# A gated attention unit and a low-rank mixer on one core: order of the start, of the first loads and of the turns of x + h

## The chip, the cores and the metric

The kernel runs on one core of one Trainium2 chip. The metric is the device time of one execution in microseconds; of several executions the median counts, and lower is better.

## The reference

Eight batches of 3136 rows; u and v have 256 columns, z has 64. All inputs and the output are float32.

```python
scores = z @ z.transpose(0, 2, 1) / 3136
attn   = np.maximum(scores, 0.0) ** 2
x      = u * (attn @ v)                                  # gated attention
h      = (x.transpose(0, 2, 1) @ U @ V).transpose(0, 2, 1)  # U: 3136 x 32, V: 32 x 3136
y      = x + h
out    = y + np.maximum(y @ w_ch1, 0.0) @ w_ch2          # w_ch1: 256 x 1024, w_ch2: 1024 x 256
```

The scores are symmetric, so a block of scores that has been computed serves a second time when it is transposed.

## The kernel before

**Tiles.** The 3136 rows of a batch are 24 tiles of 128 rows and a tail of 64. Four tiles make a group, so a batch has six whole groups (g = 0 to 5) and a small one (g = 6). An item is (batch, group), 56 in all. TensorE works in bfloat16 with the 128 rows of its array split into two halves of 64 that run at the same time (`pair`, L177; its matmuls have line 182 in the profile). PSUM is handed out as four tiles of two banks (`take_ps`, L146): a product that finds none free waits until ACT or DVE has read one.

**Scores.** The scores of group g against group J are a block of 512 x 512, made in two jobs, each one pair of matmuls (`score_pairs`, L424). ACT or DVE takes a pair out of PSUM (scale and relu, `rectify`, L364: lines 376, 382, 386, 393) and DVE squares it in place (`square`, L360, line 362; in the start ACT squares one, line 377). Blocks lie in 20 buffers (`take_block`, `give_block`). A block (J, g) with J > g is used by item g as it is, and by item J after a transpose by a DMA on SP's queue (`issue_turn`, L403: line 416, and line 408 for the half of a diagonal block). In batch 0 most are made twice instead of transposed. Which engine takes a pair is chosen by booked times (`book`, `free_at`).

**Slots.** One slot is one item's attention product with v (`av_stream`, L631, 96 units of two matmuls), with which the slot's other work is interleaved by place numbers (`emit`, L1094): score jobs of a later group (`todo`), z's turns in the start, the mixer's parts for an item seven or eight slots earlier. In slot t, x = u * (attn @ v) of item t is made (`av_out`, line 734). After a batch's last item, `t1_all` (L777, lines 782 to 796) makes x^T U for the whole batch. From then on `u2_unit` (L808) makes x + h for one item: a product with V into PSUM, the sum on DVE (line 855), a cast to bfloat16 (`down`, through `cast`, L199: line 202 on ACT, 204 on DVE), and a transpose by DMA (`turned`, `x_turn`, L767: line 770, "u2T<-x_bf"). The first channel product (`ch1_part`, L906; relu at 943 or 946) needs that transpose; the second (`ch2_stream`, L994) follows, and `ch2_out` (L1059, lines 1066 and 1068) adds and stores.

**The planner.** All of this is an instruction order worked out while the program is built. `clock` counts TensorE's planned time in units of one pair of 256 columns; `hold(due, f)` keeps a step until the planner's clock has reached `due`, and `run_held` (L122) lets out what is due. The same function then lets out block transposes from `ready_turns`, the soonest needed first, as long as `urgent` is empty and SP's booked time allows it. `urgent` holds an item whose turn of x + h shall go first; `turned` clears it. Before the change only `u2_unit` with g = 0 sets it. A product that needs a block whose transpose has not been let out issues it on the spot. Each engine executes its instructions in the order in which they were issued.

**Loads.** All DMAs go through SP's queue. z and v of the next batch are loaded in float32 into three stages and cast a slot later (`load_part`, L271; casts held in `casts_next`). U, V and the two weights are loaded once, in the slots that `first_loads` names, into attention blocks lent for it (`stage_block`); V comes in four steps of four DMAs, each weight in two steps of one. In slots 0 to 7 the loads of a slot are held 5, 27, 49, ... units after its beginning.

**The start.** z of batch 0 comes in three pieces. Each is cast twice and turned by matmuls with an identity (`z_turn`, L323, line 329), which ACT copies to `zzT` (line 338). `warm` puts matmuls of the identity on itself in front (line 327). Score pairs 0 and 1 need the first turned piece (tiles 0 to 3), pairs 2 and 3 the second (tiles 4 to 7); tiles 8 to 15 come with the third.

Of the kernel before, what the change touches and what calls it, by code (L numbers as in the profile page):

```python
# [18 lines left out]
def kernel(  # L19
# [13 lines left out]
    B, S, D = u.shape  # L33
# [10 lines left out]
    GT = 4  # L44
# [10 lines left out]
    NG = len(groups)  # L55
# [21 lines left out]
    NQ = NF // GT  # L77
# [18 lines left out]
    clock = [0.0]  # L96
# [4 lines left out]
    urgent = []  # L101
# [9 lines left out]
    def book(eng, ready, cost):  # L111
        free_at[eng] = max(free_at[eng], ready) + cost
        return free_at[eng]
# [5 lines left out]
    def hold(due, f):  # L119
        held.append((due, len(held), f))  # L120
# [18 lines left out]
    def pe(cost):  # L139
        clock[0] += cost  # L140
# [3 lines left out]
    ps_free = [0.0] * NPS  # L144

    def take_ps():  # L146
        k = min(range(NPS), key=lambda i: ps_free[i])
        assert ps_free[k] < float("inf")
        clock[0] = max(clock[0], ps_free[k])
        ps_free[k] = float("inf")  # L150
        for bank in range(2):
            wrote.pop((k, bank), None)
        return k, ps_pool.tile([P, 2, GW], FP32, name=f"ps{k}")
# [45 lines left out]
    def cast(out, in_, n):  # L199

        if free_at["act"] <= free_at["dve"]:
            nc.scalar.copy(out=out, in_=in_)  # L202
            return book("act", clock[0], n / 110)
        nc.vector.tensor_copy(out=out, in_=in_)  # L204
        return book("dve", clock[0], n / 130)
# [117 lines left out]
    def z_turn(b, t0, copy, n=2 * GT, warm=0):  # L323
        n = min(n, NT - t0)
        k, pz = take_ps()
        for _ in range(warm):
            nc.tensor.matmul(out=pz[:, 0, :P], lhsT=ident, rhs=ident, start=True, stop=True)  # L327
        for q in range(n):
            nc.tensor.matmul(  # L329
                out=pz[:, q // GT, (q % GT) * P : (q % GT + 1) * P],  # L330
                lhsT=z_bfs[b][:, t0 + q, :, :].rearrange("p c d -> p (c d)"),
                rhs=ident,
                start=(q % GT == 0),
                stop=(q % GT == GT - 1 or q == n - 1),
            )
        flat = pz.rearrange("p a c -> p (a c)")
        dst = zzTs[b].rearrange("p t c -> p (t c)")[:, t0 * P : (t0 + n) * P]
        copy(out=dst, in_=flat[:, : n * P])
        pe(8)
        ps_free[k] = book("act", clock[0] + 3, 9.5)  # L340


    def half(zzT, jj, c0, n):
# [383 lines left out]
    def four(ps):  # L727
        return ps.rearrange("p a (q d) -> p (a q) d", d=D)
# [79 lines left out]
    def u2_unit(b, g, turn=True):  # L808
        ts = tiles_of(g)
        n, t0, rows = len(ts), ts[0][1], ts[0][2]  # L810
        k, ps = take_ps()
        if n == GT:
            for a in range(2):
                pair(
                    k,
                    crossed(
                        0,
                        a,
                        lambda h, q: dict(
                            out=four(ps)[:, q, :],  # L820
                            lhsT=V4_bf[h, (t0 + q) * P : (t0 + q + 1) * P],
                            rhs=t1s[b][h, :],
                            start=(a == 0),
                            stop=(a == 1),
                        ),
                    ),
                    D,
                )
        else:
            pair(  # L830
                k,
                [
                    (
                        0,
                        0,
                        dict(
                            out=ps[:, 0, :D],
                            lhsT=V4_bf[:hp, t0 * P : (t0 + 1) * P],
                            rhs=t1s[b][:hp, :],
                            start=True,  # L840
                            stop=True,
                        ),
                    )
                ],
                D,
            )
        x = xs[b, g][:rows, :n, :]
        if b == B - 1:
            entry, raw = stage_block()
            o_blocks[b, g] = entry  # L850
            o = raw.rearrange("p (q d) -> p q d", d=D)
        else:
            o = pool.tile([P, GT, D], FP32, name="out_sb", bufs=3)
        done = ps_free[k] = book("dve", clock[0] + 3, 11.2 * n / GT)
        nc.vector.tensor_tensor(out=o[:rows, :n, :], in0=four(ps)[:rows, :n, :], in1=x, op=ALU.add)  # L855
        u2s[b, g] = o
        if not turn:
            return

        def turned():  # L860
            u2Ts[b, g] = u2T_tile()
            x_turn(b, g, u2Ts[b, g])
            urgent.clear()

        def down():
            hold(cast(x, o[:rows, :n, :], n * D) + 2, turned)

        if g == 0:
            urgent.append((b, g))
            nc.vector.tensor_copy(out=x, in_=o[:rows, :n, :])  # L870
            hold(book("dve", done, 6.3) - 6, turned)
        else:
            hold(done - 3, down)
# [293 lines left out]
    def load_w(k):  # L1167
        def step(i):
            entry, raw = stage_block()
            if k == 0:  # L1170
                nc.sync.dma_start(out=raw, in_=moe_w_ch1[i * P : (i + 1) * P, :])
                dst = w1_bf[:, i, :]
            else:
                nc.sync.dma_start(
                    out=raw.rearrange("p (t d) -> p t d", d=D),
                    in_=moe_w_ch2.rearrange("(t p) d -> p t d", p=P)[:, i * GT : (i + 1) * GT, :],
                )
                dst = w2_bf[:, i * GT : (i + 1) * GT, :].rearrange("p t d -> p (t d)")
            queued(GT * D / 2)

            def casts(entry=entry, raw=raw, dst=dst):
                cast(dst, raw, GT * D)
                give_block(entry)

            return [casts]

        return [lambda i=i: step(i) for i in range(2)]


    def load_V(i0):  # L1190
        n = P // 4

        def step(i):
            entry, raw = stage_block()
            w = n * NF + (S - NF * P if i == 3 else 0)
            for c in range(NREP):
                nc.sync.dma_start(out=raw[c * R : (c + 1) * R, :w], in_=moe_V[:, i * n * NF : i * n * NF + w])  # L1197
                queued(w / 8)

            def casts(i=i, entry=entry, raw=raw):  # L1200
                cast(
                    V4_bf[:, : NF * P].rearrange("r (t p) -> r t p", p=P)[:, :, i * n : (i + 1) * n],
                    raw[:, : n * NF].rearrange("r (p t) -> r t p", t=NF),
                    2 * n * NF,
                )
                if i == 3:
                    nc.vector.memset(V4_bf[:, S:], 0.0)
                    cast(V4_bf[:, NF * P : S], raw[:, n * NF : n * NF + S - NF * P], 100)
                give_block(entry)

            return [casts]

        return [lambda i=i: step(i) for i in range(i0, i0 + 2)]


    first_loads = {
        1: lambda: load_V(0),
        2: lambda: load_V(2),
        3: lambda: [load_U],
        4: lambda: load_w(0),  # L1220
        5: lambda: load_w(1),
    }


# [5 lines left out]
    on_act, on_dve, on_pool = nc.scalar.copy, nc.vector.tensor_copy, nc.gpsimd.tensor_copy  # L1230
# [51 lines left out]
    k, ps = take_ps()  # L1282
# [6 lines left out]
        cast_z(0, c, on_dve, GT, 2 * GT)  # L1289
    for i in range(2):  # L1290
        give_block(zraw[i][2])
    clock[0] = 38
    z_turn(0, 0, on_act, GT)
    z_turn(0, GT, on_act, GT)
    clock[0] = 43
    free_at.update(dve=46, act=47)
    jobs0 = jobs_of(0, 0)
    score_burst(jobs0[:1])
    score_burst(jobs0[1:2])
    clock[0] = 56  # L1300
    z_turn(0, 2 * GT, on_act, warm=10)
    score_burst(jobs0[2:3])
    score_burst(jobs0[3:4])
    clock[0] = 72

    todo = {t: [] for t in range(n_items)}
    for b in range(B):
        for g in range(NQ):
            t = b * NG + g - 1
# [12 lines left out]
            else:  # L1322
                todo[t] += new

    for t, most in ((0, 15), (1, 16), (2, 13)):
        todo[t + 1] = todo[t][most:] + todo[t + 1]
        todo[t] = todo[t][:most]

# [5 lines left out]
    for t in range(n_items):  # L1334
# [6 lines left out]
        g_now = t % NG  # L1341
        b_next = t // NG + 1
# [6 lines left out]
            xTs[direct] = take_block()[1][:, : GT // 2, :].rearrange("p a (q d c) -> p (a q) d c", d=ND, c=P)  # L1349
            x_turn(*direct, xTs[direct])  # L1350
        for i, f in enumerate(casts_next):
            hold(clock[0] + (90 if g_now == NQ else 15 if t > NG else 45) + 12 * i, f)
        casts_next = []
        spare += spare_next
        spare_next.clear()
        steps = first_loads[t]() if t in first_loads else []
        if b_next < B:
            steps += load_part(b_next, g_now)

        def load(step):  # L1360
            casts_next.extend(step())
# [35 lines left out]
        if av and full:  # L1397
# [5 lines left out]
            n = len(mine) - 3  # L1403
            qs += [(9 + 74 * i / n, 1, False, lambda: scores(1)) for i in range(n)]
        elif av:
# [5 lines left out]
            k = min(2, len(mine) // 3)  # L1411
            n = len(mine) - 3 * k
            at = [1 + 80 * i / n for i in range(n)]
            if t == 0:
                at, k = [14, 30, 44, 50, 64, 68, 78, 84, 92], 0
# [101 lines left out]
```

## Time and profile before

| | |
|---|---|
| median of three runs | 986.9 us (986.28 to 986.96) |
| the profiled execution | 988.19 us, span 986.4 us |
| PE (matmul) busy | 974.8 us, 99% of the span |
| DVE, ACT, POOL busy | 627.8, 483.6, 16.6 us |
| packets of the hardware DMA queue | 86.9% of 16 engines' span |
| granted TensorE clock | 1.0 |

PE is the matmul engine, PEld its weight loads, DVE the vector engine, ACT the scalar engine, SP the engine whose queue issues the DMAs. Lines of the profile carry the line of the kernel that issued an instruction, and what it writes and reads as out<-in, buffer numbers left out. A row of the timeline begins with the start and the duration in us; in brackets stands the idle time of the engine before it and what ended that. An SP row of a DMA is the time that its issue took, not its transfer. In this trace slot 0 begins near 9 us, slots 1 to 6 near 26, 44, 56, 69, 84 and 94 us, slot 7 near 96 us and slot 8 near 112 us; then a slot takes some 17 us.

### The profile page before, as it was taken

To read this page: it belongs to the slowest core of one execution; us is meant where nothing else is said; L and a number is where in the kernel's file an instruction comes from. 1 tells how busy PE (TensorE), PEld (TensorE's weight loads), DVE (VectorE), ACT (ScalarE), POOL (GpSimd) and SP (SyncE) were. 2 spreads that over 40 slices of the span, in tenths; PEclk is the share of its full clock that TensorE was granted. 3 is DMA by queue.
4 is the path that set the end of the run, shared out by engine and by line. 5 is a ranking of instruction groups with operands and counts; after the bars stand their busy time and mean duration, and the time that the engine had idled before them with its cause. 6 is when DMAs were issued, how large, how long until landed. Compare 5 with 4: busy or idle time off the path is not lost.

```text
span 986.4 us, 35362 instructions
## 1 busy us (share of the span) xinstructions
PE 974.8 (99%) x16165; PEld 780.2 (79%) x16165; DVE 627.8 (64%) x809; ACT 483.6 (49%) x562; POOL 16.6 (2%) x25
## 2 busy tenths in 40 slices
PE   9999999999999999999999999999999999999998
PEld 6798788877778778787777877788777887778766
DVE  7877755668556685567755667566775567653363
ACT  7887732456324573345633555334554346431353
POOL 4100000000000000000000000000000000000000
PEclk9999999999999999999999999999999999999999
DMA  9999999979997699897999679997899878954143
GB/s 264 208 252 181 205 205 199 197 155 190 203 192 174 151 196 217 205 151 171 180 224 209 135 178 195 227 184 137 171 214 224 179 136 167 193 121 100 49 113 99
DMA packets 372405, 176.37 MB, mean 179 GB/s; under 512 B 347296, under 2 KB 350624, under 8 KB 372256
## 3 DMA queue, kind: packets, MB, share of 16 engines
q1 hardware_dynamic: 372256, 174.12, 86.9%
q8 instruction: 126, 2.06, 0.9%
q14 instruction: 23, 0.19, 0.1%
HBM read 62.56 MB, written 25.69 MB: 89 GB/s over the span
## 4 chain that ended last, share of the span: by engine, by line
PE 94%; DVE 2%; ACT 2%; DMA 1%; SPq 1%; issue 0%; DVEq 0%; POOL 0%; POOLq 0%
PE ps L182 91%; DVE blk L362 1%; PE ps L701 1%; DMA u2T<-x_bf 1%; ACT blk L386 1%; PE ps L782 1%; PE ps L1080 0%; SPq L416 0%; DVE blk L382 0%; PE ps L1284 0%; ACT blk L946 0%; PE ps L329 0%; SPq L1197 0%; PE ps L327 0%; DVE x_bf L734 0%
## 5 line engine op out<-in xcount | busy, mean ns | idle before, releaser
L182 PEld LDWEIGHTS <-blk 64*128 64x128 bf16 x12288 | 615.6, 94 | 153.6 <-POOLq L172 9.9
L182 PE MATMUL ps<-v_bf,blk 64*128 64x256 bf16 x9216 | 612.1, 269 | 1.9 <-ACT v_bf L202 1.8
L386 ACT ACTIVATE blk<-ps 128x1024 bf16<-128x1024 f32 (+1 forms) x334 | 314.8, 972 | 346.4 <-PE ps L182 341.6
L362 DVE TENSOR_TENSOR blk<-blk 128x1024 bf16<-128x1024 bf16 x351 | 223.1, 660 | 46.8 <-ACT blk L386 46.1
L182 PE MATMUL ps<-u2T,w_bf 64*128 64x512 bf16 (+1 forms) x1792 | 227.8, 349 | 1.6 <-DMA u2T<-x_bf 1.5
L182 PE MATMUL ps<-w_bf,blk 64*128 64x256 bf16 x3072 | 192.4, 269 | 0.2 <-ACT blk L946 0.2
L943 DVE TENSOR_SCALAR blk<-ps 128x1024 bf16<-128x1024 f32 x105 | 128.5, 1224 | 94.5 <-PE ps L182 93.9
L946 ACT ACTIVATE blk<-ps 128x1024 bf16<-128x1024 f32 x87 | 88.3, 1022 | 118.3 <-PE ps L182 118.0
L182 PE MATMUL ps<-zzT 64*128 64x512 bf16 (+2 forms) x902 | 130.8, 328 | 1.3 <-ACT blk L386 0.5
L182 PEld LDWEIGHTS <-w_bf 64*128 64x128 bf16 x1792 | 84.6, 94 | 28.8 <-POOLq L172 5.0
L734 DVE TENSOR_TENSOR x_bf<-ps,u_sb 128x1024 bf16<-128x1024 f32 x48 | 58.6, 1222 | 72.3 <-PE ps L182 72.2
L855 DVE TENSOR_TENSOR out_sb<-ps,x_bf 128x1024 f32<-128x1024 f32 x42 | 51.4, 1223 | 59.5 <-PE ps L182 59.5
L1066 DVE TENSOR_TENSOR out_sb<-ps,out_sb 128x1024 f32<-128x1024 f32 x42 | 51.4, 1224 | 18.7 <-PE ps L182 18.3
L182 PEld LDWEIGHTS <-zzT 64*128 64x128 bf16 x902 | 41.8, 94 | 7.3 <-issue 2.7
L382 DVE TENSOR_SCALAR blk<-ps 128x1024 bf16<-128x1024 f32 (+1 forms) x14 | 16.1, 1147 | 11.0 <-PE ps L182 10.1
L182 PE MATMUL ps<-t_sb,V_bf 64*128 64x256 bf16 x200 | 20.6, 269 | 0.0
L204 DVE CAST v_bf<-stage 128x1024 bf16<-128x1024 f32 (+1 forms) x33 | 20.2, 611 | 0.0
L182 PE MATMUL ps<-v_bf,last_sb 64*128 64x256 bf16 x192 | 18.5, 269 | 0.2 <-POOLq L172 0.2
L202 ACT CAST v_bf<-stage 128x1024 bf16<-128x1024 f32 x15 | 15.6, 1043 | 0.0
L204 DVE CAST x_bf<-out_sb 128x1024 bf16<-128x1024 f32 x21 | 14.5, 688 | 0.3
L202 ACT CAST x_bf<-out_sb 128x1024 bf16<-128x1024 f32 x14 | 14.5, 1037 | 0.0
L362 DVE TENSOR_TENSOR attn_small<-attn_small 128x1600 bf16<-128x1600 bf16 x8 | 7.9, 991 | 9.0 <-ACT attn_small L591 9.0
(80 smaller groups left out, 240.6 us busy)
## 6 DMA issues: line engine op xcount, KB each, us to landing
u_sb<-in_u_dram SPq DMA_DIRECT2D x48, 512.0 KB, 5.2
stage<-in_v_dram SPq DMA_DIRECT2D x42, 512.0 KB, 6.2
out_dram<-out_sb SPq DMA_DIRECT2D x42, 512.0 KB, 3.1
stage<-in_z_dram SPq DMA_DIRECT2D x7, 512.0 KB, 6.1
blk<-in_v_dram SPq DMA_DIRECT2D x5, 512.0 KB, 6.1
out_dram<-blk SPq DMA_DIRECT2D x5, 512.0 KB, 2.6
blk<-blk SPq DMA_TRANSPOSE x156, 5.1
blk<-in_moe_w_ch_dram SPq DMA_DIRECT2D x4, 512.0 KB, 4.7
```

Of the source, the lines that this page charges most:

```text
L182: ins = nc.tensor.matmul(**args)
L202: nc.scalar.copy(out=out, in_=in_)
L204: nc.vector.tensor_copy(out=out, in_=in_)
L362: nc.vector.tensor_tensor(out=a, in0=a, in1=a, op=ALU.mult)
L382: nc.vector.tensor_scalar(out=dst, in0=src, scalar1=scale, scalar2=0.0, op0=ALU.mult, op1=ALU.max)
L386: nc.scalar.activation(out=dst, in_=src, func=AF.Relu, scale=scale)
L701: nc.tensor.matmul(out=ps[c * hp : c * hp + rows, h, :D], lhsT=smalls[b][h * hp : (h + 1) * hp, place_of(jt), :], rhs=v_bfs[b][h * hp : (h ...
L734: nc.vector.tensor_tensor(out=xs[b, g][:rows, :n, :], in0=four(box["ps"])[:rows, :n, :], in1=u_sbs[b, g][:rows, :n, :], op=ALU.mult,)
L855: nc.vector.tensor_tensor(out=o[:rows, :n, :], in0=four(ps)[:rows, :n, :], in1=x, op=ALU.add)
L943: nc.vector.tensor_single_scalar(out=r, in_=ps[:, :, :gw], scalar=0.0, op=ALU.max)
L946: nc.scalar.activation(out=r, in_=ps[:, :, :gw], func=AF.Relu)
L1066: nc.vector.tensor_tensor(out=o, in0=acc, in1=o, op=ALU.add)
```

## The change

It has five edits, all to the order of issue or to the planner's numbers; what is computed and each instruction's shape stay.

- `u2_unit`: an item with g > 0 now also enters `urgent` when its sum is cast, until its turn has been issued; block transposes are held back for that time.
- The start: pairs 2 and 3 are issued ahead of z's third turn; its ten warm matmuls go, and four are put ahead of the second turn. The planner counts a short turn as short.
- `first_loads`: V's two pairs of steps move from slots 1 and 2 to 3 and 4, U from 3 to 2, the weights from 4 and 5 to 5 and 6. Within a slot v's loads go ahead of them.
- Casts of what was loaded a slot before: in slot 6 from 90 to 15 units after the slot's beginning, in slot 7 from 45 to 15.
- The score jobs at most issued in slots 0, 1 and 2: 15, 16, 13 become 14, 15, 14; what is over goes to the next slot.

```diff
@@ z_turn @@
-        pe(8)
-        ps_free[k] = book("act", clock[0] + 3, 9.5)
+        pe(n)
+        ps_free[k] = book("act", clock[0] + 3, 9.5 * n / (2 * GT))
@@ u2_unit @@
         def down():
+            urgent.append((b, g))
             hold(cast(x, o[:rows, :n, :], n * D) + 2, turned)
@@ first_loads @@
-        1: lambda: load_V(0),
-        2: lambda: load_V(2),
-        3: lambda: [load_U],
-        4: lambda: load_w(0),
-        5: lambda: load_w(1),
+        2: lambda: [load_U],
+        3: lambda: load_V(0),
+        4: lambda: load_V(2),
+        5: lambda: load_w(0),
+        6: lambda: load_w(1),
@@ the start @@
-    clock[0] = 38
+    clock[0] = 32
     z_turn(0, 0, on_act, GT)
-    z_turn(0, GT, on_act, GT)
+    z_turn(0, GT, on_act, GT, warm=4)
     clock[0] = 43
     free_at.update(dve=46, act=47)
     jobs0 = jobs_of(0, 0)
     score_burst(jobs0[:1])
     score_burst(jobs0[1:2])
-    clock[0] = 56
-    z_turn(0, 2 * GT, on_act, warm=10)
     score_burst(jobs0[2:3])
     score_burst(jobs0[3:4])
-    clock[0] = 72
+    clock[0] = 58
+    z_turn(0, 2 * GT, on_act)
+    clock[0] = 68
...
-    for t, most in ((0, 15), (1, 16), (2, 13)):
+    for t, most in ((0, 14), (1, 15), (2, 14)):
         todo[t + 1] = todo[t][most:] + todo[t + 1]
         todo[t] = todo[t][:most]
...
         for i, f in enumerate(casts_next):
-            hold(clock[0] + (90 if g_now == NQ else 15 if t > NG else 45) + 12 * i, f)
+            hold(clock[0] + (90 if g_now == NQ and b_next > 1 else 15 if t >= NQ else 45) + 12 * i, f)
...
-        steps = first_loads[t]() if t in first_loads else []
-        if b_next < B:
-            steps += load_part(b_next, g_now)
+        steps = load_part(b_next, g_now) if b_next < B else []
+        steps += first_loads[t]() if t in first_loads else []
```

## The prediction

> **What bounds the kernel now.** I read the page first, then the chain of work that ended last, then the list of waits of PE, then the stretches that these two point to. The page gives the engines' shares:
>
> ```profile
> PE 974.8 (99%) x16165; PEld 780.2 (79%) x16165; DVE 627.8 (64%) x809; ACT 483.6 (49%) x562; POOL 16.6 (2%) x25
> ```
>
> PE stands idle for 986.4 - 974.8 = 11.6 us in all, so the change can only take from these and from what PE does slowly. The chain, in order of time (start, duration, what):
>
> ```profile
> 16.68 2.86 ACT blk L386 x3
> ...
> 45.32 31.15 PE ps L182 x542
> ...
> 127.02 5.45 DMA u2T<-x_bf
> ...
> 250.50 4.57 DMA u2T<-x_bf
> ...
> 351.83 89.80 PE ps L182 x1460
> ...
> 471.65 89.80 PE ps L182 x1460
> ```
>
> From 16.7 to 45 us the chain runs over ACT and DVE, afterwards over PE with a few breaks. From 351.83 on it repeats to the hundredth: 471.65 - 351.83 = 119.82 us a batch. There the change has nothing to win. What it can win lies before 256 us, and the waits of PE (total, times, longest) name it:
>
> ```profile
> PE ps L182 <- ACT v_bf L202: 1.8, 1, 1.8
> PE ps L182 <- DMA u2T<-x_bf: 1.5, 2, 0.9
> ...
> PE ps L327 <- ACT blk L376: 0.7, 1, 0.7
> ```
>
> Between 260 us and the end the same view holds one wait, of 0.2 us. In the start PE's losses hide in short gaps. I compare PE's matmuls in 11 to 46 us with those in 46 to 81 us, where that view shows no wait (groups by form; the first two rows of each):
>
> ```profile
> L182 PE MATMUL ps<-v_bf,blk 64*128 64x256 bf16 x416 | 28.9, 270 | 0.1
> L182 PE MATMUL ps<-zzT 64*128 64x512 bf16 x70 | 12.9, 376 | 1.1 <-ACT blk L386 0.5 <-DVE x_bf L734 0.5
> ...
> L182 PE MATMUL ps<-v_bf,blk 64*128 64x256 bf16 x531 | 33.1, 269 | 0.0
> L182 PE MATMUL ps<-zzT 64*128 64x512 bf16 x48 | 8.4, 376 | 0.0
> ```
>
> Counted in matmuls of 256 columns (one of 512 is two), the first 35 us hold 416 + 2 x 70 and 17 in small groups, 573; the second 531 + 2 x 48 and 20, 647. At the second's pace 573 take 31.0 us, so 4.0 us are lost between 11 and 46 us.
>
> **A. Score pairs ahead of z's second turn (start).** Rows of the timeline:
>
> ```profile
> 6.42 1.22 PE L327 MATMUL ps<-ident 128*128 128x128 bf16 x10 [0.69 <-ACT blk L376]
> ...
> 7.44 1.06 PE L329 MATMUL ps<-ident,z_bf 128*128 128x128 bf16 x8
> ...
> 8.53 1.01 ACT L338 CAST zzT<-ps 128x1024 bf16<-128x1024 f32 x1 [1.08 <-PE ps L329]
> ...
> 14.17 0.62 PE L329 MATMUL ps<-ident,z_bf 128*128 128x128 bf16 x8
> ```
>
> Ten idle matmuls (10 x 0.107 = 1.07 us) go, four come earlier (0.43 us). Pairs 2 and 3 need only z's first half and now follow pair 1 directly, so ACT goes on after its square (ends 7.46) instead of standing for 1.08 us. ACT then has two relus (0.94 each in a row) ahead of z's copy: 7.46 + 1.88 + 0.95 = 10.3 us for the copy's end, against 9.54 now. The attention stream can begin at about 8.2 (POOL's cast of v ends then) instead of 9.26, but its first score pair over z's second half has to wait for that copy: 10.4 instead of 10.93 now. Gain 0.5 us, between 0 (the copy later still) and 1.4 (the stream's own 1.06 us and some of PE's slow matmuls).
>
> On these slow matmuls: eight equal ones take 1.06 us at 7.44 and 0.62 us at 14.17, and the timeline's pace doubles near 10.8 us, 4.3 us after PE began to run without a longer gap (6.42). Idle matmuls taken out could put that off; it is the third rival. [...]
>
> **B. One score pair fewer in each of slots 0 and 1.** The limits 15, 16, 13 become 14, 15, 14: two pairs leave the stretch up to 45 us. A pair costs 0.94 us of ACT and 0.66 us of DVE (rows of 12 relus in 11.29 us, 11 squares in 8.37 us), 1.6 us over two engines that are both on the chain: 0.8 us a pair, 1.6 us for both, of the 4.0 us lost. They land in slots 2 and 3, where PE has no wait and four V casts leave. But item (0,1) begins with one finished pair less, and it already waits for squares at 28.5 to 29.7 (0.7 us on PE's weight loads). I take 1.4 us; between 0 and 2.5.
>
> **C. V two slots later, U one earlier, weights one later.** V issues 16 DMAs (3.78 us of SP's queue at 26.36, 4.99 us at 44.25), two casts of 2.10 us on ACT, two of 1.11 us on DVE and small ones. They go into slots 3 to 5, 57 to 94 us. SP's queue has holes there, 69.7 to 75.0 and 80.0 to 83.8; the casts lay at 46.8 to 64.4 without a wait of PE anywhere from 47 to 100 us. So 0; without that cover a 2.1 us cast keeps PSUM tiles from PE, and I allow 1.0 us. V is first used at 100.2 us. U's two issues (1.03 us) and casts (1.0 us) are as free. The blocks that V held are free earlier, which can only help.
>
> **D. v cast sooner.** The row, and SP's queue before it:
>
> ```profile
> 88.50 7.25 SPq L416 DMA_TRANSPOSE blk<-blk  x2
> ...
> 108.61 1.05 PE L182 MATMUL ps<-v_bf,blk 64*128 64x256 bf16 x16 [1.77 <-ACT v_bf L202]
> ```
>
> The cast of v's piece 5 is due 114 units (90 + 24) after slot 6 begins and moves to 15; a unit is a pair of 256 columns, 0.107 us, so it comes about 10 us sooner and the 1.8 us go. In their place stands the first half of w2. It is loaded in slot 6, behind its small stage, and cast 15 units into slot 7: about 17 units, 1.8 us apart. On SP it goes behind the two turns at 88.50, so at 95.8; a weight load takes 4.5 us to land in this stretch: 100.3. The cast is queued about where ACT is done with t_up, 98.9. So ACT (or DVE) waits 1.4 us, up to 2.5 when DMA is as full as here, and behind it are the relus that give PSUM tiles back, with x + h of item (0,0) after them. Of this I charge PE 0.9 us, between 0 and 2.8. D brings 1.8 - 0.9 = 0.9 us. What is late next: the turn of (0,0), issued at 103.33, lands 7.2 us later at 110.5, and its first matmul is at 112.3; once PE is 1.8 us earlier there is no slack left.
>
> **E. Right of way.** SP's queue, where PE waited at 132.5 and 255.1:
>
> ```profile
> 121.09 3.50 SPq L416 DMA_TRANSPOSE blk<-blk  x1
> ...
> 127.02 1.44 SPq L770 DMA_TRANSPOSE u2T<-x_bf  x1
> ...
> 242.98 7.43 SPq L416 DMA_TRANSPOSE blk<-blk  x2
> ```
>
> Their casts end at 122.7 and 245.0 on ACT; what is between is one block turn each, let out while the cast ran (2.3 us at 124.7; the second of the pair at 242.98, 7.43 - 5.15 = 2.3 us). The new rule holds these back, so the x turns go 2.3 us earlier, and the waits of 0.6 and 0.9 us go: 1.4 of 1.5 us, since D pulls PE forward against the first. Behind the x turn now wait the block turns and, on SP, the stores and loads after them, by its 1.2 to 1.5 us and at most the cast's remainder. Following the planner's queue, two or three turns a batch, 19 in all, are let out in that window; their blocks are read one to five slots later, and a slot lasts some 17 us. Cost 0; a bound of 1.5 us over the batches.
>
> **Sum.** 0.5 + 1.4 + 0 + 0.9 + 1.4 = 4.2 us. The profiled execution took 988.19 us (span 986.4), 1.3 above the median of the three runs, 986.9; taken off each, 984.0 and **982.7**. All ends good: 1.4 + 2.5 + 1.8 + 1.5 = 7.2, so 979.7. All bad: D at -1.0, C and E at +1.0 and +1.5, A, B at 0, E's waits kept: 990.4.
>
> **Rivals.** *First, w2's cast takes back what v's gave*: ACT stands 2.5 us at 99, u2 of (0,0) finds no PSUM tile, and its turn lands after 112.3. D then is -0.7 and the sum 2.6: 984.3. For it: 1.8 us between issue and cast, 4.5 to land. Against: four PSUM tiles, and ACT's idle 1.2 us at 101.7. *Second, nothing new appears*: w2 lands in time or its wait is hidden, and the start keeps most of its 4.0 us: some 980. *Third, the slow pace lasts longer*: PE stands before the copy that ends at 10.3, and its 4.3 us of unbroken work begin anew at 10.4, so the pace doubles at 14.7 instead of 10.8. 3.9 us at half pace cost 2.0 us, A turns to -1.5, B comes later on the same engines and brings 0.5: the sum is 1.3, 985.6. For it: the missing ten; against: four stand in for them, and the four pairs keep PE busier from 4.7 on than now. *Fourth, slower: the x turn at the head of SP's queue.* It waits there for its cast, with block turns behind it that could have gone. If a turn held back lands after the stream that reads it arrives, PE waits in every batch; 19 such turns at 0.5 us are 9.5 us, less 4.2: 992.2. It decides from a delay of over one slot, some 17 us; the x turn's longest wait in SP's waits is 7.1 us. That speaks against it.
>
> **Numbers.** Forecast 0.50 (981 to 984.2), first 0.19, second 0.13, third 0.08, fourth 0.07, and 0.03 that the edits do not bite in the issue order. This kernel's measurement can tell about 0.2%, 2 us. Faster: forecast, second, and two thirds of the first, 0.76; within 0.2%: the rest of the first, the third, and the edits without bite, 0.16; slower: the fourth and bits of the first, 0.08. The range goes from 979.6 to 986.8: the second at its best, the third at its worst.
>
> **What would show it.** No PE wait on v_bf near 108 and on u2T near 132 and 255; z's copy of 1.01 us ending near 10.3, the first score pair over z's second half near 10.4; the matmul count in 11 to 46 us above 573; the batches after 350 us still 119.8 us apart. An ACT or DVE cast of w_bf near 99 with a wait on a DMA before it decides for the first rival; matmuls at 0.107 us beyond 11 us for the third; a batch longer than 119.9 us for the fourth, and then the forecast is wrong in sign.

## The result, and the profile after

The changed kernel takes 984.97 us (median of 22 executions, 982.85 to 988.84); the kernel before took 987.26 us in the same comparison (22 executions, 984.88 to 989.61). The ratio is 0.9985, with a 95% interval from 0.9978 to 0.9992: 1.5 us faster, between 0.8 and 2.2. The forecast was 4.2. The profiled execution took 986.95 us, with a span of 985.2, 1.2 less than the span before.

The engines' shares, first; PE stands 985.2 - 973.5 = 11.7 us, as long as before (11.6):

```profile
PE 973.5 (99%) x16159; PEld 782.4 (79%) x16159; DVE 628.0 (64%) x810; ACT 481.3 (49%) x561; POOL 16.3 (2%) x25
```

The waits of PE (total, times, longest):

```profile
PE ps L182 <- ACT blk L386: 3.2, 1, 3.2
PE ps L182 <- ACT zzT L338: 1.4, 1, 1.4
...
PE ps L182 <- DVE blk L362: 0.4, 1, 0.4
```

The waits on v_bf (1.8) and u2T (1.5) are gone, as forecast. Two new ones, 4.6 us together, have taken their place and that of three shorter ones (0.7 on L376, 0.5 each on L386 and on x_bf): 3.2 us on a relu of ACT, and 1.4 us on the copy of z's third turn (zzT, line 338). The chain of work that ended last puts the first of them at 97 us, behind a weight load, and shows that the batches have not moved (470.42 - 350.59 = 119.83):

```profile
97.25 5.30 DMA blk<-in_moe_w_ch_dram
...
350.59 89.79 PE ps L182 x1460
...
470.42 89.80 PE ps L182 x1460
```

The timeline around the first wait, ACT's rows and then PE's. ACT is done with t_up at 99.0 and stands 3.57 us at the head of its queue before w2's cast; seven relus are behind it (6.09 us from 103.64); PE finds no PSUM tile and stands 3.23 us:

```profile
98.64 0.37 ACT L794 COPY t_up<-ps 64x256 f32<-64x256 f32 x1
102.57 1.05 ACT L202 CAST w_bf<-blk 128x1024 bf16<-128x1024 f32 x1 [3.57 <-DMA blk<-in_moe_w_ch_dram]
...
104.29 0.39 PE L182 MATMUL ps<-t_sb,V_bf 64*128 64x256 bf16 x4 [3.23 <-ACT blk L386]
```

The load comes late because of the queue ahead of it. SP's rows (issue start, time on the queue, what):

```profile
70.70 7.11 SPq L1198 DMA_DIRECT2D blk<-in_moe_V_dram  x8
...
82.60 4.35 SPq L416 DMA_TRANSPOSE blk<-blk  x1
...
89.78 7.38 SPq L416 DMA_TRANSPOSE blk<-blk  x2
97.25 0.86 SPq L1175 DMA_DIRECT2D blk<-in_moe_w_ch_dram  x1
```

The kernel before had a hole in this queue, from 69.7 to 75.0:

```profile
69.32 0.33 SPq L254 DMA_DIRECT2D stage<-in_v_dram  x1
74.96 1.22 SPq L408 DMA_TRANSPOSE blk<-blk  x1
```

V's eight issues now fill it and run 2.8 us past its end, and the two turns that were issued from 88.50 go from 89.78.

The timeline of the start shows the second new wait:

```profile
6.63 0.77 PE L329 MATMUL ps<-ident,z_bf 128*128 128x128 bf16 x8
7.62 1.35 PE L182 MATMUL ps<-v_bf,blk 64*128 64x256 bf16 x16 [0.23 <-ACT blk L377]
9.28 1.01 ACT L338 CAST zzT<-ps 128x1024 bf16<-128x1024 f32 x1
10.35 0.60 PE L182 MATMUL ps<-zzT 64*128 64x512 bf16 x2 [1.38 <-ACT zzT L338]
10.75 1.49 PE L182 MATMUL ps<-v_bf,blk 64*128 64x256 bf16 x12
```

The copy ends at 10.3, where the forecast had put it, and the first score pair over z's second half follows at 10.35. But the stream has nothing else to do from 8.97 on. What came behind the hole stands in the table by stretches (busy us and number of instructions on PE, PEld, DVE, ACT, POOL; then the granted clock of PE, DMA share, GB/s):

```profile
7.00:10.30 3.30, 1.62 (x23) 0.95 (x20) 2.37 (x4) 3.30 (x4) 2.00 (x3) 1.00 1.01 349
10.40:13.70 3.30, 3.30 (x28) 2.03 (x30) 2.59 (x4) 1.00 (x1) 0.37 (x1) 0.50 1.06 324
```

After a stretch in which PE was busy for 1.62 of 3.30 us, the granted clock is 0.50 from 10.4 to 13.7: 28 matmuls in 3.3 us. The kernel before ran 48 in the same stretch, at a granted clock of 1.00:

```profile
10.40:13.70 3.30, 3.30 (x48) 2.18 (x46) 3.30 (x6) 2.09 (x3) 1.60 (x3) 1.00 1.05 335
```

Where x_bf of items (0,0) and (0,1) and `t1_all` of batch 0 begin (DVE's line 734, PE's line 782) splits the first 100 us in three, for this and for the experiments' profiles:

| kernel | start | limits | V's slots | (0,0) at | then to (0,1) | then to t1_all |
|---|---|---|---|---|---|---|
| before | old | 15, 16, 13 | 1, 2 | 26.59 | 17.47 | 53.45 |
| e6_new_start_only | new | 15, 16, 13 | 1, 2 | 27.43 | 17.48 | 53.45 |
| e11_limits_only | old | 14, 15, 14 | 1, 2 | 24.83 | 16.15 | 54.90 |
| e10_old_limits | old | 15, 16, 13 | 1, 2 | 25.17 | 17.47 | 54.57 |
| e9_old_start_V_early | old | 14, 15, 14 | 1, 2 | 26.34 | 16.15 | 53.89 |
| e7_V_early | new | 14, 15, 14 | 1, 2 | 26.03 | 16.15 | 53.88 |
| after | new | 14, 15, 14 | 3, 4 | 27.22 | 16.08 | 53.45 |
| e5_changed_again | new | 14, 15, 14 | 3, 4 | 25.97 | 16.09 | 53.44 |
| e2_old_start | old | 14, 15, 14 | 3, 4 | 24.87 | 16.09 | 53.45 |

Three readings rest on it. The new limits take 1.3 to 1.4 us off the way from (0,0) to (0,1), whatever else is changed. With V in slots 1 and 2, a part of that can be lost again between (0,1) and t1_all (0.44 us in e7 and e9, 1.45 in e11, against the 53.45 of before); with V in 3 and 4 nothing is. The limits are not what decides it: e10 has the old ones and loses 1.12. There ACT casts V twice (2.09 us each, at 47.66 and 50.56), and PE then waits 0.94 us for a relu, at 53.63; in e7 and e9 DVE makes both casts near there. And the new start is the later one: 26.0 or 27.2 to 27.4, against 24.8 to 25.2 or 26.3 to 26.6. Each start has two values, by how much of it ran at half pace: between 7.0 and 10.3 us the old one did 29 matmuls in the profile before and 51 in e2's, and between 10.4 and 13.7 us the new one did 28 in the changed kernel's and 46 in e5's.

### The profile page after: what moved, and what is told of

Read it like the earlier page. It is cut to its first block, busy times and chain, and to the rows that moved or that the text cites. A ratio compares the mean times of both kernels' runs of the same rounds, so it can differ in the third digit from the quotient of the medians.

```text
span 985.2 us, 35363 instructions
## 1 busy us (share of the span) xinstructions
PE 973.5 (99%) x16159; PEld 782.4 (79%) x16159; DVE 628.0 (64%) x810; ACT 481.3 (49%) x561; POOL 16.3 (2%) x25
## 4 chain that ended last, share of the span: by engine, by line
PE 96%; DMA 2%; SPq 1%; DVE 0%; ACT 0%; issue 0%; POOL 0%; DVEq 0%; ACTq 0%; POOLq 0%
PE ps L182 94%; PE ps L701 1%; DMA blk<-in_v_dram 1%; PE ps L782 1%; DMA blk<-in_moe_w_ch_dram 1%; DMA stage<-in_v_dram 0%; PE ps L1081 0%; ACT blk L947 0%; POOL v_bf L1246 0%; SPq L1259 0%; SPq L218 0%; SPq L224 0%; DVE x_bf L734 0%; SPq L254 0%; DVE blk L722 0%
## 5 line engine op out<-in xcount | busy, mean ns | idle before, releaser
L386 ACT ACTIVATE blk<-ps 128x1024 bf16<-128x1024 f32 (+1 forms) x334 | 314.3, 972 | 343.1 <-PE ps L182 340.2
L362 DVE TENSOR_TENSOR blk<-blk 128x1024 bf16<-128x1024 bf16 (+1 forms) x350 | 222.3, 660 | 50.2 <-ACT blk L386 49.5
L182 PEld LDWEIGHTS <-w_bf 64*128 64x128 bf16 x1792 | 85.3, 94 | 26.3 <-POOLq L172 5.0
L202 ACT CAST v_bf<-stage 128x1024 bf16<-128x1024 f32 (+1 forms) x17 | 17.0, 1002 | 0.0
L182 PEld LDWEIGHTS <-V_bf 64*128 64x128 bf16 x200 | 10.5, 94 | 5.8 <-issue 3.4
L1067 DVE TENSOR_TENSOR blk<-ps,blk 128x1024 f32<-128x1024 f32 x5 | 6.1, 1223 | 11.6 <-PE ps L182 11.6
```

The lines of the kernel that those rows point to most:

```text
L182: ins = nc.tensor.matmul(**args)
L362: nc.vector.tensor_tensor(out=a, in0=a, in1=a, op=ALU.mult)
L386: nc.scalar.activation(out=dst, in_=src, func=AF.Relu, scale=scale)
L1067: nc.vector.tensor_tensor(out=o, in0=acc, in1=o, op=ALU.add)
```

## The experiments

Theory: the forecast's missing 2.7 us went into two places, z's copy in the start with the slower clock behind it, and w2's cast behind SP's full queue. Rivals: w2's wait only takes over a wait that would come anyway; the right of way, or V's new slots, cost something elsewhere. All ratios are to the kernel before on the same chip (median 986.2 to 986.9).

**e1_w2_late.** The changed kernel, with w2's first cast held until late in slot 7:

```diff
-            hold(clock[0] + (90 if g_now == NQ and b_next > 1 else 15 if t >= NQ else 45) + 12 * i, f)
+            hold(clock[0] + (90 if g_now == NQ and b_next > 1 or t == NG else 15 if t >= NQ else 45) + 12 * i, f)
```

> The changed kernel, with the cast of w2's first half held 90 units into slot 7 instead of 15. Theory (w2's cast took the gain back): PE's wait of 3.2 us at 104.3 us for ACT's relu, behind a cast that waits 3.6 us for its DMA, is gone, no wait on v_bf comes back at 108, and the time falls by some 3 us below the changed kernel, 4.5 us below the kernel before. Rival (SP's queue sets slots 7 and 8 anyway): the wait only moves to the first channel product near 112 us, for the turn of x + h of item (0,0), and the time falls by less than 1.5 us.

Measured: 984.29 us, ratio 0.9989 [0.9980, 0.9998]; no gain over the changed kernel. PE's wait on ACT is gone, and another stands a few us later, in the timeline of PE:

```profile
111.20 0.61 PE L182 MATMUL ps<-u2T,w_bf 64*128 64x512 bf16 x4 [1.47 <-DMA u2T<-x_bf]
```

The turn of (0,0) was issued at 104.00, as soon as its cast ended (103.97), and landed at 111.2, after 7.2 us, as long as in the kernel before. So freeing ACT alone does not bring the gain: the next to be waited for is the x turn, for which the prediction had seen no slack left. Why w2 is late, this run does not say.

**e2_old_start.** The changed kernel with the start of the one before:

```diff
-        pe(n)
+        pe(8)
...
-    clock[0] = 32
+    clock[0] = 38
-    z_turn(0, GT, on_act, GT, warm=4)
+    z_turn(0, GT, on_act, GT)
...
+    clock[0] = 56
+    z_turn(0, 2 * GT, on_act, warm=10)
     score_burst(jobs0[2:3])
     score_burst(jobs0[3:4])
-    clock[0] = 58
-    z_turn(0, 2 * GT, on_act)
-    clock[0] = 68
+    clock[0] = 72
```

> The changed kernel with the start of before: z's third turn with ten warm matmuls ahead of score pairs 2 and 3, and the planner's numbers that go with it; all else as changed. Theory (the new start costs): PE's wait of 1.4 us for z's copy near 10 us is gone, item (0,0) ends some 0.6 us sooner than in the changed kernel, and the time is 0.5 to 2 us below the changed kernel's. Rival (the new start is where the gain is): the time is 0.5 to 1.5 us above the changed kernel's, and gaps come back between 38 and 46 us.

Measured: 982.55 us, ratio 0.9964 [0.9951, 0.9976], 2 us below the changed kernel's 0.9985. Neither new wait is in its profile, so it removed both at once: (0,0) came at 24.87, V's eight issues of one step took 4.42 us of SP's queue instead of 7.11, and w2 went out at 91.56 instead of 97.25:

```profile
68.49 4.42 SPq L1198 DMA_DIRECT2D blk<-in_moe_V_dram  x8
...
91.56 0.54 SPq L1175 DMA_DIRECT2D blk<-in_moe_w_ch_dram  x1
```

V sits in slots 3 and 4 here too. SP stood free again from 77.78 to 80.09, and w2 was issued 4.7 us ahead of ACT's t_up (96.30); in the changed kernel it was 1.4 us (98.64).

**e3_right_of_way.** The kernel before with `urgent.append((b, g))` in `down` and nothing else.

> The kernel before with one line more: an item with g over 0 also enters urgent. Theory: both waits on u2T (132 and 255 us, 1.5 us together) go and nothing else changes: 1.5 us below the kernel before, the batches after 350 us 119.8 us apart. Rival (block turns held back cost): the two waits go, but the gain is under 0.5 us or a batch takes longer than 119.9 us.

Measured: 984.92 us, ratio 0.9990 [0.9981, 0.9999], 1.0 us faster. Both waits on u2T are gone, the one on v_bf stays at 1.8, and the batches stand 119.83 apart. The right of way costs nothing that can be seen.

**e4_warm_in_hole.** The changed kernel with eight idle matmuls ahead of z's third turn:

```diff
-    z_turn(0, 2 * GT, on_act)
+    z_turn(0, 2 * GT, on_act, warm=8)
```

> The changed kernel with eight warm matmuls ahead of z's third turn; PE stands 1.4 us for z's copy soon after, so they should take no time of their own. Theory (the hole lets the array's clock fall back for 3.4 us): the matmuls after 10.4 us run at 0.107 us a pair at once, item (0,0) ends 1 us sooner, and the time is 1 to 1.7 us below the changed kernel's. Rival (ACT and DVE set the pace there): PE is faster but waits more, and the time is within 0.3 us of the changed kernel's.

Measured: 983.17 us, ratio 0.9969 [0.9958, 0.9981]. The granted clock was 1.00 behind the hole, with 46 matmuls between 10.4 and 13.7 us (as in e5's, e7's and e12's profiles, without the eight), and all six executions had a mean granted clock of 0.999 or 1.0. But the wait on z's copy was still 1.0 us, and w2's wait, which the edit does not touch, had gone too. So this run alone does not say which of the two brought the gain; e13 does.

**e5_changed_again.** The changed kernel itself, beside the next three.

> The changed kernel as it is, beside the next three. Theory (its gain hangs on where two things fall: the array's clock window in the start, and SP's lateness before w2): 1 to 2 us below the kernel before, its executions spread over 4 us and more, and those with a granted clock of 0.997 the slowest, by some 2 us. Rival (the spread is the same for every kernel and says nothing): time and granted clock of the executions are not related.

Measured: 985.71 us, ratio 0.9997 [0.9988, 1.0006]. In its profile the granted clock was 1.00 behind the first hole (46 matmuls between 10.4 and 13.7 us) and 0.50 behind the second, of 2.45 us. The table by stretches, at the second hole (99.8 to 102.3 us):

```profile
95.00:101.00 6.00, 4.82 (x93) 3.61 (x88) 4.75 (x10) 3.16 (x5) 0.00 (x0) 1.00 1.10 213
101.90:105.20 3.30, 2.93 (x26) 2.17 (x27) 2.25 (x4) 2.52 (x4) 0.00 (x0) 0.50 1.06 376
```

The same program thus had a granted clock of 0.50 behind one hole (10.39 to 13.80 us in the changed kernel's profile) or behind the other (101.9 to 105.2 us here). Its executions differ with the clock: of the changed kernel's 33, those with a mean granted clock of 0.999 or 1.0 took 982.85 to 985.82 us; those with 0.998 or less took 985.71 to 988.84, but for one of 983.52. By estimate, those 3.41 us at 0.50 are 1.7 us of work, or 0.002 of the mean clock over a span of 985 us.

**e6_new_start_only.** The kernel before with the changed start alone (the reverse of e2's diff).

> The kernel before with the new start alone (score pairs 2 and 3 ahead of z's third turn, four warm matmuls for ten, the planner's numbers for it). Theory (the new start costs): PE waits 1 to 1.4 us for z's copy near 10 us, and the time is 0.5 to 2 us above the kernel before. Rival (as the prediction had it): 0.5 us below it.

Measured: 986.74 us, ratio 1.0007 [0.9998, 1.0016]; by itself the start gains nothing and most likely loses 0.7 us. In its profile the wait on z's copy and the half clock stand as in the changed kernel:

```profile
10.40:13.70 3.30, 3.30 (x28) 2.03 (x30) 2.72 (x5) 0.99 (x1) 0.60 (x1) 0.50 1.05 321
```

**e7_V_early.** The changed kernel, with V loaded in slots 1 and 2 again and U in 3:

```diff
-        2: lambda: [load_U],
-        3: lambda: load_V(0),
-        4: lambda: load_V(2),
+        1: lambda: load_V(0),
+        2: lambda: load_V(2),
+        3: lambda: [load_U],
```

> The changed kernel with V loaded in slots 1 and 2 and U in slot 3, as before; the weights and the casts stay as changed. Theory (V's 16 issues in slots 3 and 4 put SP's queue late, and with it w2's first half): w2's issue comes 1.5 to 3 us sooner against PE, its cast waits under 1 us, PE's wait at 104 us is gone, and the time is 1 to 2.5 us below the changed kernel's. Rival (V's place costs nothing, as the prediction had it): w2's issue and the time stay within 0.5 us, or gaps come back before 46 us and it is slower.

Measured: 983.49 us, ratio 0.9972 [0.9963, 0.9981], 2.5 us below e5 on the same chip (0.9997 - 0.9972), although the wait on z's copy stood at 1.7. SP's rows have the free stretches that the kernel before had, and w2 goes out 3.8 us sooner than in the changed kernel, 4.5 us ahead of t_up (97.95):

```profile
68.30 0.56 SPq L254 DMA_DIRECT2D stage<-in_v_dram  x1
73.56 1.20 SPq L408 DMA_TRANSPOSE blk<-blk  x1
...
93.43 0.54 SPq L1175 DMA_DIRECT2D blk<-in_moe_w_ch_dram  x1
```

PE's wait on w2 is gone; what is left is 0.4 us on the turn of (0,0). So, with the new start, V's new slots are what makes w2 late. The slots alone do not: e2 and e4 have them too, and their eight issues took 4.4 and 5.0 us and did w2 no harm.

**e8_copy_on_dve.** The changed kernel, with z's third copy on DVE (`z_turn(0, 2 * GT, on_dve)`).

> The changed kernel with z's third copy on DVE instead of ACT: DVE has a free stretch from 7.8 us, ACT gets to it only at 9.3 us. Theory (the hole of PE before that copy costs the start): the copy ends near 9.2 us instead of 10.3, the hole shrinks from 1.4 us to 0.3 us, item (0,0) ends about 1 us sooner, and the time is 1 to 2 us below the changed kernel's. Rival (the squares that DVE then does later hold PE as long): item (0,0) ends within 0.3 us of the changed kernel's.

Measured: 984.75 us, ratio 0.9992 [0.9983, 1.0001], inconclusive: its interval overlaps e5's. The wait on the copy became one of 1.6 us of the turn itself on DVE's cast of z, and w2's wait stayed at 2.2. The time of the start only changed its name.

**e9_old_start_V_early**, **e10_old_limits**, **e11_limits_only.** e9 has e2's and e7's edits; e10 is e9 with the limits 15, 16, 13; e11 is the kernel before with 14, 15, 14.

> The changed kernel with the start of before and V and U in their slots of before (1, 2 and 3): what is left of the change is the right of way, v's sooner cast, the weights one slot later and the limits 14, 15, 14. Theory (the two undone parts each cost some 2 us, through different holes of PE): neither the wait for z's copy nor that behind w2's cast is there, and the time is 4 to 5.5 us below the kernel before, lowest of all so far. Rival (the two are one effect, for instance only how late the start is): no lower than with either of them undone alone, some 3 us below.

> The kernel of the run before this one, with the limits 15, 16, 13 of before as well. Theory (two pairs fewer up to 45 us free ACT and DVE): gaps of PE come back between 38 and 46 us and the time is 1 to 1.6 us above that run's. Rival (the limits do nothing, the gaps go by the start alone): within 0.3 us.

> The kernel before with the limits 14, 15, 14 alone. Theory: PE's waits for ACT's relu and for x near 40 and 45 us (0.5 us each) go, 1 to 1.4 us below the kernel before. Rival: item (0,1) waits longer for squares near 29 us and the gain is under 0.4 us.

Measured: 983.21 us, ratio 0.9962 [0.9949, 0.9976]; 985.47, 0.9987 [0.9978, 0.9996]; 986.60, 0.9996 [0.9987, 1.0005]. e9 is no better than e2: with the old start w2's wait was gone already, so V's early slots had nothing left to bring. The limits were worth 2.5 us between e10 and e9 and 0.4 alone. The table above says why alone they bring so little: e11 wins 1.3 us before item (0,1) and loses 1.45 after it, where PE waits at 50.8 and 51.8 for relus (0.42 and 0.52 us) on an ACT that has a cast of V, of 2.13 us, in its row at 46.8. Of the 2.5 us between e10 and e9, 1.3 lie ahead of (0,1) and 0.7 behind it, where e10 has its two casts of V on ACT. By the times alone the two values are not far apart: 0.4 has an interval from -0.5 to 1.3, and 2.5 one of about 1.6 either way.

**e12_V_on_pool.** The changed kernel, with V's loads issued by POOL: `nc.gpsimd.dma_start` for `nc.sync.dma_start` at line 1198.

> The changed kernel with V's 16 loads issued on POOL's queue instead of SP's, in the same slots 3 and 4. Theory (what V costs is SP's queue, which is full from 57 to 98 us): w2's first half is issued 2 us sooner or more against PE, its cast waits under 1 us, PE's wait behind it is gone, and the time is 1.5 to 2.5 us below the changed kernel's. Rival (the DMA engines themselves are full there): SP's transposes take as long as before, w2 lands as late, and the time is within 0.5 us of the changed kernel's.

Measured: 982.79 us, ratio 0.9964 [0.9952, 0.9977]. With V off SP's queue, but in its new slots, w2 went out at 92.49 and its wait was gone. In this run, then, it is the queue and not V's casts or its bytes.

**e13_eight_later.** e4's eight idle matmuls in another place: ahead of z's last turn, at about 19 us (`z_turn(0, 6 * GT, on_act, warm=8)`), where no hole is.

> The changed kernel with the same eight warm matmuls as in the run that filled the hole, but ahead of z's last turn near 19 us, where PE has no hole. Theory (filling the hole of the start is what that run gained by): the time is that of the changed kernel or 0.4 us above, executions at a granted clock of 0.997 still appear, and PE's wait behind w2's cast near 102 us stays. Rival (eight more matmuls shift where SP's queue pauses, 2 us before V's last load, and that alone took the wait behind w2 away): the pause and the wait are gone here too, and the time is 1 to 2 us below the changed kernel's.

Measured: 983.84 us, ratio 0.9974 [0.9966, 0.9983], nearly e4's gain. The wait on z's copy stayed at 1.4, and that on w2 shrank to 0.7, because the load had been issued at 94.93. ACT's row:

```profile
99.28 1.05 ACT L202 CAST w_bf<-blk 128x1024 bf16<-128x1024 f32 x1 [1.04 <-DMA blk<-in_moe_w_ch_dram]
```

So the rival to e4's reading holds: most of e4's gain came from w2, by an earlier SP queue. What is left for filling the hole, 0.5 us (0.9974 against 0.9969), lies within the intervals. How eight matmuls free SP is only half known. The step of eight V issues takes 7.11 us on SP's queue in the changed kernel's profile, 6.9 in e1's, 6.7 in e5's, 6.5 in e8's, 5.7 here and 5.0 in e4's; of the 7.11 us, 1.85 are a pause of SP between two of them (75.65 to 77.50). SP's waits put 1.8 us of it down to a load of v (stage<-in_v_dram); that this load is the cause no run shows.

**e14_pool_old_start**, **e15_pool_warm.** e12 with e2's start, and e12 with e4's eight matmuls, for a still faster kernel.

> V's loads on POOL's queue and the start of before; all else as changed. Theory (two holes, each with a cost of its own): below either alone, 4 to 5 us below the kernel before. Rival (with w2's wait gone the start costs nothing more): within 0.5 us of V on POOL alone, 3.5 us below.

> V's loads on POOL's queue and eight warm matmuls ahead of z's third turn; all else as changed. Theory (the array's clock falls back in the hole of the start in some executions): the slowest executions of V on POOL alone disappear, the median moves by less than 0.5 us, 3.5 to 4 us below the kernel before. Rival (the hole itself is the cost, not the clock): the same spread as V on POOL alone.

Measured: ratios 1.0000 [0.9985, 1.0015] and 1.0002 [0.9986, 1.0018], over executions from 982.41 to 991.28 us; neither question got an answer. The chain of e14 shows a new loss:

```profile
65.85 13.48 DMA blk<-blk
79.38 7.21 PE ps L182 x119
86.59 2.70 issue
```

A block turn took 13.48 us to land, where the median between 66 and 100 us is 5.4 in the changed kernel; POOL's loads were in flight beside it, which does not show that they caused it. e12's five executions, 982.44 to 984.12 us, were all among the fast ones. What decides it stays open, and V on POOL is no version to keep.

**The sum over the runs.** Three groups of kernels with the new limits and the right of way, in us below the kernel before (one less the ratio, times 986.3): new start with a wait at w2 or at the x turn behind it (after 1.5, e5 0.3, e1 1.1, e8 0.8; mean 0.9); new start with V's jam on SP relieved (e4 3.1, e7 2.8, e12 3.6, e13 2.6; mean 3.0); old start and no such wait (e2 3.6, e9 3.7; mean 3.6). e14 and e15, which lose elsewhere, are left out. The jam costs 2.1 us, the start about 0.6; each single value has an interval of 0.7 to 1.3 us either way, so the first is clear of that and the second is not. The jam shows only with both the new start and V's new slots: with the old start V may sit in either place (e2 and e9). Of the versions with V on SP's queue, e2_old_start and e9_old_start_V_early have the lowest ratios: the whole change without its start beats the kernel before by 3.6 us, and by its interval the changed kernel too.

## Why the prediction was wrong, step by step

The forecast had the sign right and 2.7 us too much. Three terms hold the difference: A, C, and w2's half of D. The last two are one loss, seen where it begins and where PE meets it.

**A, the start: no gain, and most likely a loss.** Forecast +0.5, measured about -0.7 (e6: 1.0007; e2 and e9 against e4, e7, e12, e13: -0.6). Neither figure is clear of zero by itself, but e6's interval (0.9998 to 1.0016) leaves out the forecast's 0.9995, and x_bf of (0,0) comes 0.6 to 1.2 us later than with the old start, whether half pace lasted long or short. The times were right: stream from 7.6 (forecast 8.2), copy's end at 10.3, score pair at 10.35 (10.4). The step that failed is the reading of them. The step booked as a gain that the stream begins sooner and that the pair comes sooner. It did not ask what the stream does between the two: PE stands 1.4 us there, and only the third rival had this. In the old order PE was busy for all of 7.0 to 10.3, in the profile before as in e2's; in the new one for 1.62 of 3.30 us.

The third rival, to which 0.08 was given, came nearest to what the profile shows: PE stands 1.38 us before the copy, and the granted clock is 0.50 until 13.80. In the profile the clock falls rather than stays low (1.00 from 7.0 to 10.3), and 28 matmuls fit where 48 did. Its count, 4.3 us of unbroken work from 6.42 on, was the author's estimate from one execution and does not hold: e2 has the same order of start, and there 51 matmuls fit between 7.0 and 10.3 us, where the profile before has 29. In the changed kernel's profile the granted clock was 1.00 again from 13.80, where the rival had 14.7. That the gap by itself halves the clock is not shown either: after a wait of 1.4 us on the copy the granted clock was 0.50 in two profiles (after and e6) and 1.00 in e13's, after 1.0 us it was 0.52 in e1's and 1.00 in e5's.

**B, the limits: right.** Forecast 1.4, measured 1.3 to 1.4 us between (0,0) and (0,1) in every profile of the table with the new limits. That it is so close is partly luck: 1.4 was a choice between 0 and 2.5, and 11 squares in 8.37 us are 0.76 each, not 0.66. What the step did not say is that V's casts can take it back: with V in slots 1 and 2, 0.4 to 1.45 us is lost behind (0,1) in e7, e9, e10 and e11. The matmuls in 11 to 46 us, counted as the prediction did, rose from 573 to 430 + 2 x 68 + 17 = 583, as it asked, though 2.8 of these us, 11 to 13.80, ran at a granted clock of 0.50.

**C, V two slots later: the step that failed most.** It was booked at 0, because the queue had holes at 69.7 and 80.0 and no wait of PE stood near. With the old start that would have held: in e2 eight issues of 4.42 us fit into the hole, and w2 was not late. In the changed kernel's profile they took 7.11 us where 4.99 had been read from the old place, 1.85 of it a pause of SP (75.65 to 77.50). From 63.6 to 101 us the queue then had no other gap above 0.8 us, and every later issue, w2's among them, moved back. The cover was counted in DMA time and PE waits; what mattered was how long the issues take in the new place and who is next on the queue. The price, with the new start, was 2.1 us (e5 against e7: 2.5; e12 the same by another way); with the old start e2 and e9 show none. C's bound of 1.0 us had been for casts, and was for the wrong resource. Why SP pauses in some profiles and not in others stays open.

**D: v's gain right, w2's price too low.** The wait of 1.8 us on v_bf went. For w2 the prediction took the issue at 95.8 and 4.5 us to land; they were 97.25 and 5.30. ACT therefore stood 3.57 us instead of 1.4, and PE 3.23 instead of 0.9. D came to 1.8 - 3.2 = -1.4 in the profile. The first rival (ACT stands, w2's cast takes back what v's gave, -0.7, chance 0.19) was the right case, and larger. D's last sentence held too: take the cast's wait away (e1), and PE waits for the turn of (0,0) instead.

**E, the right of way: right.** Both waits on u2T went; e3 measured 1.0 us (0.1 to 1.9) against 1.4. The x turn that PE waited for at 132 goes out at 122.85 instead of 127.02. The fourth rival is out: 119.83 us a batch, in e3 as in the changed kernel.

**The terms put together**, in the profiled executions: t1_all of batch 0 begins 0.77 us sooner (A and B, where 1.9 was forecast); D adds 1.8 - 3.2, E 1.5; 0.9 us in all, and the span is 1.2 us shorter.

## What to carry to other kernels

When a step is moved on a queue that is shared, list what stands behind its new place, up to the next thing that an engine waits for, and shift that by the step's full issue time, with a margin (the same eight issues took from 4.4 to 7.1 us here); "no engine waits there now" is not cover. An order that makes one stage begin sooner and the next no sooner opens a hole on the engine that bounds the kernel, and what follows the hole can be slow too (28 matmuls in 3.3 us here, 46 in e5's profile of the same kernel). And a change of several parts is best measured by taking each part out of the whole (e2, e7, e10) as well as alone (e3, e6, e11): the limits were worth 2.5 us with the others and 0.4 without, and V's new slots 2.1 us with the new start and nothing that shows with the old.

## What the runs showed of the hardware that was not expected

In the changed kernel's profile a gap of 1.38 us on TensorE, in a stretch of 3.3 us in which it was busy for 1.62, was followed by a granted clock of 0.50 from 10.39 to 13.80 us. Neither the length of the gap nor the busy time ahead decides alone. The profiles with the new start and z's copy on ACT, with PE's busy time between 7.0 and 10.3 us and its wait on the copy (us), then the granted clock and PE's matmuls between 10.4 and 13.7:

| profile | PE busy | wait on z's copy | granted clock | matmuls |
|---|---|---|---|---|
| after | 1.62 | 1.4 | 0.50 | 28 |
| e6_new_start_only | 1.62 | 1.4 | 0.50 | 28 |
| e1_w2_late | 1.66 | 1.0 | 0.52 | 30 |
| e4_warm_in_hole | 1.77 | 1.0 | 1.00 | 46 |
| e13_eight_later | 1.36 | 1.4 | 1.00 | 46 |
| e5_changed_again | 1.33 | 1.0 | 1.00 | 46 |
| e12_V_on_pool | 1.33 | 1.0 | 1.00 | 46 |
| e7_V_early | 1.16 | 1.7 | 1.00 | 46 |

It is the same at the second hole: that of 3.23 us, from 101 to 104.3 us in the changed kernel's profile, was followed by a granted clock of 1.00 (56 matmuls between 104.3 and 107.6), and e5's of 2.45 us by one of 0.50 (26 matmuls between 101.9 and 105.2). What decides is not shown and stays open.

One program had the lower clock behind its first hole in one profile and behind its second in the other, and its executions differed by some 2 us with their mean clock (median 984.8 us at 0.999 or 1.0, 987.0 at 0.998 or less). The clock's column must be read with the matmuls beside it: for 7.0 to 10.3 it says 1.00 in the profile before as well, where 29 matmuls filled the 3.3 us that take 51 in e2's; the trace of the kernel before has no record of the clock ahead of 10.88 us. And with loads issued by POOL beside block turns, one turn took 13.48 us in e14's profile, where 5.4 is the median in the changed kernel's between 66 and 100 us; in e12's profile the median between 55 and 98 us is 5.6.
